# A gated mix of two spectral filters on one core: exchanging real and imaginary parts by DMA, gate rows from a constant column, gate sums over two engines

## The chip, the cores and the metric

The kernel runs on one core of one Trainium2 chip. The core has five engines that run their own instruction queues in order and meet at semaphores: PE (TensorE, matrix products from SBUF into PSUM), DVE (VectorE, elementwise work), ACT (ScalarE, functions and copies, here most copies out of PSUM), POOL (GpSimd, small elementwise work) and SP (SyncE, which here only issues DMAs). A DMA that an engine issues moves data on 16 shared DMA engines. PSUM has 8 banks of 512 fp32 columns, numbered 0 to 7.

The metric is the device time of one execution in microseconds (us), as the median of several runs. The profile is one further execution, recorded instruction by instruction; its span runs from the first instruction to the last.

## The reference

Two spectral filters are applied to the same input and mixed row by row with a gate:

```python
def _A_ref(x, w_r, w_i):          # _B_ref is the same
    X = rfft2(x.astype(float32), axes=(-2, -1))
    X = X * (w_r + 1j * w_i)
    return irfft2(X, s=(S, D), axes=(-2, -1)).astype(bfloat16)

x = A_x                                               # (1, 2048, 1024) bf16
g = sigmoid((x * gate_w).sum(-1, keepdims=True))      # one gate per row
return g * _A_ref(x, A_w_r, A_w_i) + (1 - g) * _B_ref(x, B_w_r, B_w_i)
```

The weights are 2048 x 513 each, real and imaginary, for A and B. Both filters share one forward transform, because their input is the same.

## The kernel before

The transform is written as matrix products with constant tables. The 2048 rows are split as 32 x 64: row 64 n1 + n2. SBUF holds 128 partitions with 16 rows of x each, so x arrives in 8 chunks of two rows per partition.

**Loads.** SP issues all large DMAs in one list (L264 to L291): table M, the chunks of x, the gate weights `gw` (one row of 1024 sent to all partitions, into RB), tables F2 and CK, and then the weights in 8 blocks W(0) to W(7) by `wblock`. Blocks 0 to 6 go to R_W, four DMAs each. Block 7 goes into R_M, over table M, in four pairs of DMAs (1539 and 513 columns); each of these lists all keys ("M", c) as written, so by the rule of `Prog.add` each waits for the one before it.

**Stage 1** (`stage1(c)`, c = 0 to 3, chunks 2c and 2c+1): transform over n1 and folding of columns. DVE copies reversed halves of x into RING (L314), PE runs 32 matmuls of 256 columns, and `evict1` (L340) takes four PSUM groups into R_F: three by ACT, the fourth, for step c-1, by DVE. A gate sum `zred(c)` (L305: x row times gate weights, summed into one column of ZS) stands on DVE in each step.

**Stages 2 and 4** are one loop over 16 slots i. `stage2(i)`: 8 matmuls of 512 columns (L378) give the spectrum along d; ACT evicts it as CS(i) into RING (L381; 3 buffers); POOL copies one column to STAR. `stage4(i)`: 8 matmuls (L399) finish the row transform twice, once with the constants in normal order (sw = 0) and once with real and imaginary columns swapped (sw = 1). ACT evicts both, X(0, i) and X(1, i), into RING (L402; 2 buffers each). Then DVE forms two products with the weights (L413), 2048 columns each: `product` for sw = 0 goes to R_A, where x has been, and for sw = 1 to R_W, over the weights of block j-1, with j = i // 2. Real and imaginary parts lie in partitions 2k and 2k+1. The program order on each engine is that of the calls: stage2(i+1), wsave on POOL for even i, stage4(i), and in iterations 0 to 5 two further `zred`.

**The gate.** `gate_diag(r)` (L355) lets POOL write the identity times column r of ZS, a 128 x 128 block of DZ; two per iteration for i below 8. `gate_rows` (called in iterations 10 and 11) multiplies them by a matrix of ones on PE (L362), which spreads each sum over all partitions, and ACT applies the sigmoid (L367) into DZ. After the loop DVE makes from it the masks GM in RING (L467).

**Stages 5 to 7.** Before stage 5, U5 replaces block 7 and F2 in R_M by a DMA; `star` and PST treat the single last column. Stage 5 (L526, 32 groups of 16 matmuls, PSUM slots of two banks used in turn, evicted by ACT and DVE alternately at L535) transforms back over the rows; it needs all products. `rbgen` (L480) makes, from U5 and GM, the right-hand sides of `stage6` (L558) in seven buffers `rbs`; `stage7` (L571) transforms back along d, DVE adds and subtracts the halves (L579), and SP stores 16 outputs.

Semaphores: `Prog.add` takes for each operation the keys it reads (r), rewrites (w: waits for all earlier readers and writers) and adds to (a: waits for earlier readers). Waits are inserted from these, and engines never reorder.

Of the kernel before, what the change touches and what calls it, by code (L numbers as in the profile page):

```python
# [205 lines left out]
def bass_gated_mix__spectral_gfnet__spectral_gfnet__prompt_kernel(nc, A_x, A_w_r, A_w_i, B_x, B_w_r, B_w_i, gate_w, out):  # L206
# [71 lines left out]
    def wblock(j):  # L278
        t, base = (R_W, 4112 * (j + 1)) if j < 7 else (R_M, 0)
        for f in range(2):  # L280
            for ri in range(2):
                w = wsrc[f, ri]
                d0 = base + 2052 * f
                if j < 7:
                    parts = [(d0, 2052, [[(29 - 4 * j) * 513, 2], [1, 1026]], 2 * j + 1)]
                else:
                    parts = [(d0, 1539, [[1, 1539]], 15), (d0 + 1539, 513, [[1, 513]], 0)]
                for do, n, dims, k in parts:
                    dma("sp", AP(t, ri * t.shape[1] + do, [[2 * t.shape[1], 64], [1, n]]),
                        AP(w.tensor, w.offset + k * 513, [[32 * 513, 64]] + dims),  # L290
                        w=[("M", c) for c in range(4)] + [("M-", c) for c in range(4)] if j == 7 else [], a=[("W", j)])  # L291
# [10 lines left out]


    def zred(r):
        P.add("dve", lambda e: e.tensor_tensor_reduce(  # L305
            out=sl(RB, 1024, [(1, 1024)]), in0=sl(R_A, XO + r * 1024, [(1, 1024)]), in1=sl(RB, GWo, [(1, 1024)]),
            scale=1.0, scalar=0.0, op0=ALU.mult, op1=ALU.add, accum_out=ZS[:, r:r + 1]),
            r=[("x", r // 2), "gw"], w=["zjunk"], a=[("z", r)])
# [45 lines left out]
    def gate_diag(r):  # L354
        P.add("pool", lambda e: e.tensor_scalar(out=sl(DZ, r * 128, [(1, 128)]), in0=sl(CK, IDo, [(1, 128)]),  # L355
                                                scalar1=ZS[:, r:r + 1], scalar2=None, op0=ALU.mult),
              r=[("z", r), "CK"], a=["DZ"])

    def gate_rows(h):
        b0 = 2 * h  # L360
        for q in range(2 * h, 2 * h + 2):
            P.add("pe", lambda e, q=q: e.matmul(ps((b0 + q % 2) * 512, [(1, 512)]), sl(CK, ONo, [(1, 128)]),  # L362
                                                sl(DZ, q * 512, [(1, 512)]), start=True, stop=True),
                  r=["DZ", "CK"], w=[bank(b0 + q % 2)])
# [21 lines left out]
    def stage4(i):  # L386
        t = order[i]
        kind = 0 if t else 1
        ro = CSO + (i % 3) * 1028
        for sw in range(2):  # L390
            b0 = 4 + 2 * sw
            for pm in range(2):
                for m in range(2):
# [5 lines left out]
                    P.add("pe", lambda e, o=o, lh=lh, rh=rh, m=m: e.matmul(o, lh, rh, start=(m == 0), stop=(m == 1)),  # L399
                          r=["CK", ("CS", i % 3)], w=[bank(b0 + pm)])  # L400
# [1 line left out]
            P.add("act", lambda e, xo=xo, b0=b0: e.activation(sl(RING, xo, [(1, 1024)]), ps(b0 * 512, [(1, 1024)]), ACT.Copy),  # L402
                  r=[bank(b0), bank(b0 + 1)], w=[("X", sw, i % 2)] + ALLX)
# [2 lines left out]
        for sw in range(2):
            xin = sl(RING, (XAO if sw == 0 else XSO) + (i % 2) * 1024, [(0, 2), (512, 2), (1, 512)])
            win = sl(wt, w0, [(2052, 2), (dpm, 2), (1, 512)])
            dst = sl(R_A if sw == 0 else R_W, 4 * i * RW, [(2 * RW, 2), (RW, 2), (1, 512)])
            free = [("x", c) for c in range(8)] if sw == 0 and i >= 8 else []  # L410
            if sw == 1 and j > 0:
                free = [("W", j - 1)]
            P.add("dve", lambda e, d=dst, a=xin, b=win: e.tensor_tensor(out=d, in0=a, in1=b, op=ALU.mult),  # L413
                  r=[("X", sw, i % 2), ("W", j)], a=[("prod", sw)] + free)
# [60 lines left out]

    def rbgen(r):
        t, so = rbs[r % 7]
        for cp in range(2):
            for ri in range(2):
# [3 lines left out]
                    in1=sl(RING, r * 256, [(64, 4), (32, 2), (1, 32)]), op=ALU.mult),  # L483
# [171 lines left out]
```

## Time and profile before

| | us |
|---|---|
| median of 3 runs | 180.57 |
| range of the runs | 179.12 to 180.71 |
| the profiled execution's own time | 180.38 |
| its span | 178.5 |

| engine | busy us | share of the span |
|---|---|---|
| PE, matmuls | 152.0 | 85% |
| DVE | 119.0 | 67% |
| ACT | 110.1 | 62% |
| POOL | 44.9 | 25% |

The profile names an instruction by its line in the kernel file (L378), its engine, and its tiles as output<-input. In a timeline a row reads: start, time from there to the end, engine, line, operation, tiles, count, and in brackets how long the engine had been idle and what ended that. In a table of groups, a row ends with total busy time, mean nanoseconds of one, and the idle time before. An instruction's duration is longer than the distance to the next where the two overlap. Time outside the span (180.38 less 178.5) belongs to the execution but to no instruction.

### The profile page before, as it was taken

How to read it: one execution, taken by the hardware profiler on the slowest of the kernel's cores; microseconds unless marked ns; L12 is line 12 of the kernel's file. 1: busy time of each engine (PE TensorE's matmuls, PEld its weight loads, DVE VectorE, ACT ScalarE, POOL GpSimd, SP SyncE). 2: the span in 40 equal slices, each digit the busy share in tenths (PEclk: the TensorE clock that was granted, in tenths of full speed). 3: DMA queues.
4: the chain of work that ended last, by engine and by line, in shares of the span. 5: the costliest groups of instructions: out<-in, count | busy, mean ns of one | idle time of the engine just before them, and what ended most of it. 6: DMA issues, size and time to landing. Idle time of an engine off the chain costs nothing. (4 is left out here: it accounts for less than half of the span.)

```text
span 178.5 us, 3235 instructions
## 1 busy us (share of the span) xinstructions
PE 152.0 (85%) x1295; PEld 99.0 (55%) x1308; DVE 119.0 (67%) x192; ACT 110.1 (62%) x121; POOL 44.9 (25%) x55
## 2 busy tenths in 40 slices
PE   0789969999997723999985799999978999999991
PEld 0568834444442201344434799999966666656640
DVE  0168722999999992055779277888852787765463
ACT  4359837888876660498992545476556665565550
POOL 0000005899999997001014000000000000000000
PEclk9999999999999996599997899999999999999999
DMA  5999999991221000000003900000051313322323
GB/s 161 300 417 431 400 383 387 389 379 39 59 56 51 15 0 0 0 4 2 0 0 62 385 26 4 0 4 0 4 174 64 118 62 120 118 87 93 118 112 124
DMA packets 9295, 22.97 MB, mean 129 GB/s; under 512 B 1216, under 2 KB 1600, under 8 KB 8896
## 3 DMA queue, kind: packets, MB, share of 16 engines
q1 hardware_dynamic: 9136, 22.76, 34.9%
q8 instruction: 10, 0.16, 0.4%
q14 instruction: 5, 0.04, 0.1%
q10 hardware_dynamic: 144, 0.00, 0.0%
HBM read 18.57 MB, written 4.19 MB: 127 GB/s over the span
## 5 line engine op out<-in xcount | busy, mean ns | idle before, releaser
L402 ACT ACTIVATE RING<-PS 128x1024 bf16<-128x1024 f32 x32 | 32.8, 1024 | 7.4 <-DVE R_A L413 3.8
L399 PE MATMUL PS<-RING,CK 128*128 128x512 bf16 (+1 forms) x123 | 31.2, 384 | 3.0 <-ACT RING L402 2.6
L526 PE MATMUL PS<-CK,R_A 128*128 128x128 bf16 x256 | 32.4, 228 | 1.2 <-DVE R_A L413 1.2
L526 PE MATMUL PS<-CK,R_W 128*128 128x128 bf16 x256 | 32.3, 228 | 0.9 <-DVE R_W L413 0.9
L378 PE MATMUL PS<-R_M,R_F 128*128 128x512 bf16 x127 | 31.6, 395 | 1.6 <-issue 1.6
L526 PEld LDWEIGHTS PS<-CK,R_A 128*128 128x128 bf16 x256 | 31.4, 145 | 1.3 <-DVE R_A L413 1.3
L526 PEld LDWEIGHTS PS<-CK,R_W 128*128 128x128 bf16 x256 | 31.4, 145 | 1.0 <-DVE R_W L413 1.0
L579 DVE TENSOR_TENSOR R_A<-R_A,PS 128x512 bf16<-128x512 f32 x32 | 20.6, 684 | 15.3 <-ACT R_A L575 10.0
L571 PE MATMUL PS<-R_A 128*128 128x512 bf16 x121 | 29.2, 379 | 0.9 <-DMA R_A<-c_DI 0.6
L413 DVE TENSOR_TENSOR R_A<-RING,R_W 128x2048 bf16<-128x2048 bf16 x14 | 17.2, 1231 | 18.6 <-ACT RING L402 18.6
L355 POOL TENSOR_SCALAR DZ<-CK,ZS 128x128 bf16<-128x128 bf16 x16 | 29.3, 1839 | 0.0
L562 ACT ACTIVATE R_A<-PS 128x1024 bf16<-128x1024 f32 x16 | 16.3, 1024 | 16.7 <-PE PS L558 16.7
L399 PEld LDWEIGHTS PS<-RING,CK 128*128 128x128 bf16 x128 | 12.1, 99 | 20.3 <-ACT RING L402 6.3
L378 PEld LDWEIGHTS PS<-R_M,R_F 128*128 128x128 bf16 x128 | 12.9, 101 | 17.8 <-issue 3.8
L332 PE MATMUL PS<-R_M,R_A 128*128 128x256 bf16 x64 | 16.3, 298 | 6.3 <-DVE RING L314 5.6
L305 DVE CUSTOM_DVE_ANT_0 RB<-R_A,RB 128x1024 bf16<-128x1024 bf16 x16 | 19.8, 1235 | 2.8 <-DMA RB<-in_gate_w_dram 2.6
L381 ACT ACTIVATE RING<-PS 128x1024 bf16<-128x1024 f32 x16 | 16.5, 1029 | 7.5 <-PE PS L378 6.6
L571 PEld LDWEIGHTS PS<-R_A 128*128 128x128 bf16 x128 | 11.9, 98 | 12.3 <-DMA R_A<-c_DI 0.5
L383 POOL COPY STAR<-RING 128x1 bf16<-128x1 bf16 x16 | 6.8, 426 | 46.9 <-ACT RING L381 46.9
L413 DVE TENSOR_TENSOR R_W<-RING,R_W 128x2048 bf16<-128x2048 bf16 x14 | 17.5, 1250 | 0.0
L332 PE MATMUL PS<-R_M,RING 128*128 128x256 bf16 x64 | 16.3, 298 | 0.0
L535 ACT ACTIVATE R_F<-PS 128x1024 bf16<-128x1024 f32 x8 | 8.2, 1024 | 10.4 <-PE PS L526 10.4
(55 smaller groups left out, 167.5 us busy)
## 6 DMA issues: line engine op xcount, KB each, us to landing
R_A<-in_A_x_dram SPq DMA_DIRECT2D x8, 512.0 KB, 8.8
out_dram<-R_A SPq DMA_DIRECT2D x16, 256.0 KB, 2.0
R_M<-c_U SPq DMA_DIRECT2D x1, 2048.0 KB, 7.6
R_W<-in_A_w_r_dram SPq DMA_DIRECT2D x7, 256.5 KB, 10.8
R_W<-in_A_w_i_dram SPq DMA_DIRECT2D x7, 256.5 KB, 10.4
R_W<-in_B_w_r_dram SPq DMA_DIRECT2D x7, 256.5 KB, 9.6
R_W<-in_B_w_i_dram SPq DMA_DIRECT2D x7, 256.5 KB, 9.7
R_M<-c_F SPq DMA_DIRECT2D x1, 1024.0 KB, 13.4
```

Of the source, the lines that this page charges most:

```text
L305: P.add("dve", lambda e: e.tensor_tensor_reduce(out=sl(RB, 1024, [(1, 1024)]), in0=sl(R_A, XO + r * 1024, [(1, 1024)]), in1=sl(RB, GWo, [( ...
L332: P.add("pe", lambda e, o=o, lh=lh, rh=rh, h=h: e.matmul(o, lh, rh, start=(h == 0), stop=(h == 1)), r=[("x", 2 * c + q // 2), ("M", c), (" ...
L355: P.add("pool", lambda e: e.tensor_scalar(out=sl(DZ, r * 128, [(1, 128)]), in0=sl(CK, IDo, [(1, 128)]), scalar1=ZS[:, r:r + 1], scalar2=No ...
L378: P.add("pe", lambda e, o=o, lh=lh, rh=rh, j=j: e.matmul(o, lh, rh, start=(j == 0), stop=(j == 3)), r=["F1", "F2"], w=[bank(b0 + cs)])
L381: P.add("act", lambda e: e.activation(sl(RING, ro, [(513, 2), (1, 512)]), ps(b0 * 512, [(512, 2), (1, 512)]), ACT.Copy), r=[bank(b0), bank ...
L399: P.add("pe", lambda e, o=o, lh=lh, rh=rh, m=m: e.matmul(o, lh, rh, start=(m == 0), stop=(m == 1)), r=["CK", ("CS", i % 3)], w=[bank(b0 + ...
L402: P.add("act", lambda e, xo=xo, b0=b0: e.activation(sl(RING, xo, [(1, 1024)]), ps(b0 * 512, [(1, 1024)]), ACT.Copy), r=[bank(b0), bank(b0 ...
L413: P.add("dve", lambda e, d=dst, a=xin, b=win: e.tensor_tensor(out=d, in0=a, in1=b, op=ALU.mult), r=[("X", sw, i % 2), ("W", j)], a=[("prod ...
L526: P.add("pe", lambda e, o=o, t=t, l0=l0, ab=ab: e.matmul(o, sl(t, l0, [(257, 128)]), sl(CK, KIAo if ab == 0 else KIBo, [(1, 128)]), start= ...
L562: P.add("act", lambda e, s=src, d=dst: e.activation(d, s, ACT.Copy), r=[bank(b0), bank(b0 + 1)], w=[("Y", r)], after=[last5])
L571: P.add("pe", lambda e, o=o, lh=lh, rh=rh, q=q: e.matmul(o, lh, rh, start=(q == 0), stop=(q == 3)), r=[("Y", r), "DI"], w=[bank(b0 + ri)])
L579: P.add("dve", lambda e, od=od, h=h: e.tensor_tensor(out=od, in0=es, in1=ps((b0 + 1) * 512, [(1, 512)]), op=ALU.add if h == 0 else ALU.sub ...
```

## The change

- **Exchange.** In iterations 0 to 14, stage 4 runs only sw = 0. The swapped copy is made by two DMAs on SP, SBUF to SBUF: odd partitions of XA(i) to even partitions of XS(i) and the reverse, 64 partitions of 1024 columns each. XA has 4 buffers in RING, XS has 3, in RB and DZ. Iteration 15 still computes both on PE. PSUM banks 4 to 7 alternate by iteration.
- **Order of the products.** `product(0, i)` stays in iteration i; `product(1, i-2)` follows it, two iterations after its exchange. The loop ends with (1,13), (0,15), (1,15), (1,14).
- **Weight loads.** `wloads` lists 32 loads (block, filter, part). The first 20 (blocks 0 to 4) are issued ahead of the loop; then two loads in each of iterations 0 to 5, behind the exchange of that iteration on SP.
- **Gate sums.** For rows 0 to 11, DVE multiplies x by the gate weights in place (`zpair`, two rows at a time, in stage 1's steps 1 to 3), and ACT sums each row with a Copy that has an accumulator output (`zsum`): three ahead of stage 2, nine inside the loop after the XA eviction of iterations 0, 1, 3, 4, 6, 7, 9, 10 and 12. Rows 12 to 15 keep the fused sum on DVE, now in place, after stage 1.
- **Gate rows.** The diagonals on POOL are gone. DVE copies ZS to ZB in bf16 after product(1,12); PE multiplies a column of ZB, read with step 0 as a 128 x 128 stationary operand, by the identity, 16 matmuls of 128 columns; the four sigmoids write into RING. All of it stands behind the loop, after XST.
- **Start.** A memset on DVE and ten matmuls of 512 columns on the zeros stand ahead of stage 1. The gate weights are loaded before chunk 1 of x, where they were loaded before chunk 2.
- **Buffers.** `rbs` uses other places, GM lies at column 2056 of RING, and stage 5 starts with PSUM slot 2 where it started with slot 1. Frees of x by the products go by the chunks they overlap.

```diff
-        if c == 2:
+        if c == 1:
             dma("sp", sl(RB, GWo, [(1, 1024)]), AP(gate_w.tensor, gate_w.offset, [[0, 128], [1, 1024]]), w=["gw"])
...
-    def wblock(j):
+    def wload(j, f, ri):
...
+            dma("sp", AP(t, ri * t.shape[1] + do, [[2 * t.shape[1], 64], [1, n]]),
+                AP(w.tensor, w.offset + k * 513, [[32 * 513, 64]] + dims),
+                w=[("M", c) for c in range(4)] + [("M-", c) for c in range(4)] if j == 7 else [], a=[("W", j)])
+
+    wloads = [(j, f, ri) for j in range(8) for f in range(2) for ri in range(2)]
...
+    P.add("dve", lambda e: e.memset(sl(R_F, 0, [(1, 512)]), 0.0), w=["F1"])
+    for n in range(10):
+        P.add("pe", lambda e: e.matmul(ps(3584, [(1, 512)]), sl(R_F, 0, [(1, 128)]), sl(R_F, 0, [(1, 512)]), start=True, stop=True),
+              r=["F1"], w=[bank(7)])
+
+    def zpair(k):
+        xs = sl(R_A, XO + k * 2048, [(1024, 2), (1, 1024)])
+        P.add("dve", lambda e: e.tensor_tensor(out=xs, in0=xs, in1=sl(RB, GWo, [(0, 2), (1, 1024)]), op=ALU.mult),
+              r=["gw"], w=[("x", k)])
+
+    def zsum(r):
+        xs = sl(R_A, XO + r * 1024, [(1, 1024)])
+        P.add("act", lambda e: e.activation(xs, xs, ACT.Copy, accum_out=ZS[:, r:r + 1]), r=[("x", r // 2)], a=["z"])
...
             evict1(c - 1, 3, "dve")
-        zred(c)
+            zpair(2 * c - 2)
+            zpair(2 * c - 1)
...
-    for j in range(8):
-        wblock(j)
+    for r in range(12, 16):
+        zred(r)
+    for n in range(20):
+        wload(*wloads[n])
...
+    def gate_rows():
+        for q in (1, 2, 3, 0):
+            for r in range(4 * q, 4 * q + 4):
+                P.add("pe", lambda e, r=r: e.matmul(ps(r * 128, [(1, 128)]), sl(ZB, r, [(0, 128)]), sl(CK, IDo, [(1, 128)]),
+                                                    start=True, stop=True), r=["ZB", "CK"], w=[bank(q)])
+            src = ps(q * 512, [(128, 4), (1, 4), (4, 32)])
+            P.add("act", lambda e, q=q, s=src: e.activation(sl(RING, q * 512, [(1, 512)]), s, ACT.Sigmoid, scale=SM[:, 0:1]),
+                  r=[bank(q), "SM"], a=["G"] + [("CS", i) for i in range(3)])
...
-        for sw in range(2):
-            b0 = 4 + 2 * sw
+        xo = XAO + (i % 4) * 1024
+        xt, xs = xsb[i % 3]
+        for sw in range(2 if i == 15 else 1):
+            b0 = 4 + 2 * ((i + sw) % 2)
...
+        if i < 15:
+            for ri in range(2):
+                src = AP(RING, (1 - ri) * RING.shape[1] + xo, [[2 * RING.shape[1], 64], [1, 1024]])
+                dst = AP(xt, ri * xt.shape[1] + xs, [[2 * xt.shape[1], 64], [1, 1024]])
+                dma("sp", dst, src, r=[("XA", i % 4)], w=[("XS", i % 3)] if ri == 0 else [], a=[("XS", i % 3)] if ri else [])
...
+    zat = {0: 3, 1: 4, 3: 5, 4: 6, 6: 7, 7: 8, 9: 9, 10: 10, 12: 11}
+    for r in range(3):
+        zsum(r)
     stage2(0)
     for i in range(16):
-        if i in (10, 11):
-            gate_rows(i - 10)
         if i + 1 < 16:
             stage2(i + 1)
         if i % 2 == 0:
             wsave(i // 2)
         stage4(i)
-        if i < 6:
-            zred(4 + 2 * i)
-            zred(5 + 2 * i)
-        if i < 8:
-            gate_diag(2 * i)
-            gate_diag(2 * i + 1)
+        if i in zat:
+            zsum(zat[i])
+        for n in range(20 + 2 * i, min(22 + 2 * i, 32)):
+            wload(*wloads[n])
+        if i == 15:
+            product(1, 13)
+        product(0, i)
+        if i >= 2:
+            product(1, i - 2 if i < 15 else 15)
+        if i == 14:
+            P.add("dve", lambda e: e.tensor_copy(ZB[:], ZS[:]), r=["z"], w=["ZB"])
+    product(1, 14)
...
-    slot = 1
+    slot = 2
```

More of the change, by code (lines that the diff above doesn't have):

```diff
@@ L275, in bass_gated_mix__spectral_gfnet__spectral_gfnet__prompt_kernel @@
               r=[("M", c)], w=[("M-", c)])
-    def wblock(j):
+    def wload(j, f, ri):
         t, base = (R_W, 4112 * (j + 1)) if j < 7 else (R_M, 0)
[L280 to L291, printed above, removed]
+        w = wsrc[f, ri]
+        d0 = base + 2052 * f
+        if j < 7:
+            parts = [(d0, 2052, [[(29 - 4 * j) * 513, 2], [1, 1026]], 2 * j + 1)]
+        else:
+            parts = [(d0, 1539, [[1, 1539]], 15), (d0 + 1539, 513, [[1, 513]], 0)]
+        for do, n, dims, k in parts:
+            dma("sp", AP(t, ri * t.shape[1] + do, [[2 * t.shape[1], 64], [1, n]]),
+                AP(w.tensor, w.offset + k * 513, [[32 * 513, 64]] + dims),
+                w=[("M", c) for c in range(4)] + [("M-", c) for c in range(4)] if j == 7 else [], a=[("W", j)])
+    wloads = [(j, f, ri) for j in range(8) for f in range(2) for ri in range(2)]
     def wrow(j, a):
@@ L400, in stage4 @@
                           r=["CK", ("CS", i % 3)], w=[bank(b0 + pm)])
-            xo = (XAO if sw == 0 else XSO) + (i % 2) * 1024
-            P.add("act", lambda e, xo=xo, b0=b0: e.activation(sl(RING, xo, [(1, 1024)]), ps(b0 * 512, [(1, 1024)]), ACT.Copy),
-                  r=[bank(b0), bank(b0 + 1)], w=[("X", sw, i % 2)] + ALLX)
+            dst, key = (sl(RING, xo, [(1, 1024)]), ("XA", i % 4)) if sw == 0 else (sl(xt, xs, [(1, 1024)]), ("XS", i % 3))
+            P.add("act", lambda e, d=dst, b0=b0: e.activation(d, ps(b0 * 512, [(1, 1024)]), ACT.Copy),
+                  r=[bank(b0), bank(b0 + 1)], w=[key] + ALLX)
@@ L404, in stage4, with product @@
+        if i < 15:
[3 more added lines that the diff above has]
+                dma("sp", dst, src, r=[("XA", i % 4)], w=[("XS", i % 3)] if ri == 0 else [], a=[("XS", i % 3)] if ri else [])
+    def product(sw, i):
         j = i // 2
         wt, w0, dpm = wrow(j, i % 2)
[L406 to L414, printed above, removed]
+        xt, xo = (RING, XAO + (i % 4) * 1024) if sw == 0 else xsb[i % 3]
+        xin = sl(xt, xo, [(0, 2), (512, 2), (1, 512)])
+        win = sl(wt, w0, [(2052, 2), (dpm, 2), (1, 512)])
+        dst = sl(R_A if sw == 0 else R_W, 4 * i * RW, [(2 * RW, 2), (RW, 2), (1, 512)])
+        free = []
+        if sw == 0 and i >= 8:
+            k0, k1 = (max(0, 4 * i * RW - XO) // 2048, ((4 * i + 4) * RW - 1 - XO) // 2048)
+            free = [("x", k) for k in range(k0, k1 + 1)]
+        if sw == 1 and j > 0:
+            free = [("W", j - 1)]
+        P.add("dve", lambda e: e.tensor_tensor(out=dst, in0=xin, in1=win, op=ALU.mult),
+              r=[("XA", i % 4) if sw == 0 else ("XS", i % 3), ("W", j)], a=[("prod", sw)] + free)
@@ L482, in rbgen @@
                     in0=sl(R_M, r * 512 + cp * 64 + ri * 32, [(128, 4), (0, 2), (1, 32)]),
[L483 removed]
+                    in1=sl(RING, GMo + r * 256, [(64, 4), (32, 2), (1, 32)]), op=ALU.mult),
                     r=["U5", "GM"], w=[("RB", r % 7, cp, ri)], a=rbk[r] if r < 7 else [])
```

32 lines of the change are left out of this document (11 added, 21 removed).

## The prediction, made before the changed kernel was run

> **What bounds the kernel now.** I read first the table by stretches, because the mean over the span (PE 85% busy) hides a stage in which the engine at the limit changes. Columns: stretch, its length, busy time of PE, PEld, DVE, ACT and POOL, granted clock, DMA share, GB/s.
>
> ```profile
> span 178.5 us, 3235 instructions
> 31.00:48.40 17.40, 17.29 (x80) 7.87 (x81) 17.26 (x23) 15.46 (x16) 16.70 (x12) 1.00 0.62 224
> 48.40:63.00 14.60, 12.50 (x56) 4.89 (x55) 14.53 (x18) 9.75 (x11) 14.60 (x12) 1.00 0.15 42
> 63.00:70.00 7.00, 0.56 (x3) 0.07 (x1) 5.28 (x5) 2.66 (x3) 7.00 (x7) 0.89 0.00 0
> 70.00:77.00 7.00, 6.99 (x21) 2.69 (x22) 0.12 (x1) 3.36 (x5) 0.95 (x7) 0.62 0.00 0
> 77.00:93.50 16.50, 15.70 (x71) 6.80 (x72) 11.36 (x10) 15.14 (x16) 1.40 (x8) 1.00 0.01 1
> ```
>
> The loop of stages 2 and 4 runs from 24 to 96 us. PE, DVE and POOL are all nearly full up to 48, then DVE and POOL are; from 63 to 70 PE stands still, and from 70 to 77 it works at a granted clock of 0.62; after that PE and ACT are full together. The timeline, engine by engine, says why:
>
> ```profile
> 63.66 5.01 POOL L355 TENSOR_SCALAR DZ<-CK,ZS 128x128 bf16<-128x128 bf16 x2
> 70.01 1.04 PE L362 MATMUL PS<-DZ,CK 128*128 128x512 bf16 x2 [6.45 <-POOL DZ L355]
> 70.84 3.62 PE L378 MATMUL PS<-R_M,R_F 128*128 128x512 bf16 x8
> 80.38 1.89 PE L378 MATMUL PS<-R_M,R_F 128*128 128x512 bf16 x8
> 83.83 1.89 PE L378 MATMUL PS<-R_M,R_F 128*128 128x512 bf16 x8
> 88.07 1.23 DVE L413 TENSOR_TENSOR R_A<-RING,R_W 128x2048 bf16<-128x2048 bf16 x1 [1.05 <-ACT RING L402]
> 89.21 1.22 DVE L413 TENSOR_TENSOR R_W<-RING,R_W 128x2048 bf16<-128x2048 bf16 x1
> 90.43 4.44 ACT L402 ACTIVATE RING<-PS 128x1024 bf16<-128x1024 f32 x4
> 94.91 1.22 DVE L413 TENSOR_TENSOR R_W<-RING,R_M 128x2048 bf16<-128x2048 bf16 x1
> 96.18 0.32 PE L526 MATMUL PS<-CK,R_W 128*128 128x128 bf16 x1 [0.87 <-DVE R_W L413]
> ```
>
> PE waits 6.45 us for POOL's diagonals, then runs its next eight matmuls in 3.62 us where eight take 1.89. Undisturbed, an iteration of 16 matmuls is 83.83 − 80.38 = 3.45 us, so one 512-column matmul is 0.216. A product is 89.21 − 88.07 = 1.14 apart, an ACT eviction (4.44 − 1.02)/3 = 1.14. Stage 5 starts when the last product ends (96.13); from 96.18 to the end of the span, 82.3 us, PE bounds and the change touches only a buffer and a bank number.
>
> **The change part by part.**
>
> *Removed.* Half of stage 4 in 15 of 16 iterations: 60 matmuls (13 us of PE), 15 evictions (17 us of ACT). The 16 diagonals on POOL with the wait above. PE needs 12 × 0.216 = 2.6 us an iteration, DVE two products, 2.3, ACT two evictions plus, in 9 iterations, a gate sum. So ACT becomes the busiest engine of the loop, until something waits.
>
> *Start of the loop.* DVE now does two 2048-wide gate products (zpair) in each of stage 1's steps 1 to 3, where it did one gate sum.
>
> ```profile
> 11.99 0.43 DVE L314 COPY RING<-R_A 128x1024 bf16<-128x1024 bf16 x1 [0.85 <-DMA R_A<-in_A_x_dram]
> 12.34 1.22 DVE L340 CAST R_F<-PS 128x1024 bf16<-128x1024 f32 x1
> 13.47 1.21 DVE L305 CUSTOM_DVE_ANT_0 RB<-R_A,RB 128x1024 bf16<-128x1024 bf16 x1
> 14.61 0.76 DVE L314 COPY RING<-R_A 128x1024 bf16<-128x1024 bf16 x2
> 22.95 1.22 DVE L340 CAST R_F<-PS 128x1024 bf16<-128x1024 f32 x1 [1.13 <-PE PS L332]
> 24.49 3.40 PE L378 MATMUL PS<-R_M,R_F 128*128 128x512 bf16 x15 [1.58 <-issue]
> 20.33 2.85 ACT L340 ACTIVATE R_F<-PS 128x1024 bf16<-128x1024 f32 x3 [0.64 <-PE PS L332]
> ```
>
> No row shows zpair; the product of the same size and kind gives 1.15. From the fourth chunk of x (its copy starts at 11.99, on a DMA) DVE has no gap any more: 12.35, then twice (eviction 1.14 + zpair 2.3 + copies 0.78), then 1.14 + 2.3, then the last eviction 1.22: 25.4 instead of 24.17. PE starts stage 2 at 25.7, ACT is free of stage 1 at 24.3 instead of 23.2. The four gate sums left to DVE then run to 30.4 and are hidden, since no product can start before 31.6.
>
> The ten warm-up matmuls and the memset cost and gain nothing: step 1 waits for the chunk at 11.99 however fast step 0 was. Moving the gate-weight load forward delays x's second chunk by about 2 us at most, hidden by the same wait (exposed, 2 us).
>
> *Gate sums on ACT.* No row shows an ACT sum. Bounds from rows:
>
> ```profile
> L274 ACT ACTIVATE R_M<-R_M 128x512 bf16<-128x512 bf16 x4 | 2.3, 622 | 4.1 <-DMA R_M<-c_M 4.1
> L263 ACT ACTIVATE JNK<-JNK 128x1 f32<-128x1 f32 x1 | 0.2, 202 | 0.0
> L402 ACT ACTIVATE RING<-PS 128x1024 bf16<-128x1024 f32 x32 | 32.8, 1024 | 7.4 <-DVE R_A L413 3.8 <-DVE R_W L413 0.4 <-PE PS L399 0.3
> L305 DVE CUSTOM_DVE_ANT_0 RB<-R_A,RB 128x1024 bf16<-128x1024 bf16 x16 | 19.8, 1235 | 2.8 <-DMA RB<-in_gate_w_dram 2.6
> ```
>
> 1024 columns take 1.02; a separate read of the accumulator would be a [128x1] instruction of up to 0.20, partly overlapped. Low end 1.0, high end 1.4, taken 1.2. In the Trainium skill, ScalarE: Activation LUTs, the rules for kernel authors say that multiplications and additions belong on VectorE rather than ScalarE, and the section on what a table load costs prices an ACTIVATE at 186 ns + 0.833 ns per column. As an estimate from that page an ACT sum is 1.04 us without the accumulator, and the sum below would come 1 us lower. The rule speaks against this edit, and the rows agree with it: a sum was 1.24 on DVE and is now 0.57 + 1.2 over both.
>
> An XA eviction waits for two DMAs more than before. 1.14 is the low end, taken 1.25, high end 1.36, since these evictions with several waits already stand 1.14 apart where stage 1's three in 2.85 stand 0.92 apart.
>
> ACT: three sums from 24.3 to 27.9, CS0 and CS1 to 30.3, XA0 to 31.6 (after PE's first two stage 2 and stage 4); then up to XA4's end 3 sums, 4 CS and 4 XA, 3.6 + 4.6 + 5.0 = 13.2: XA4 is ready at 44.7.
>
> *Exchange and weight loads share SP's queue.* This decides the result. An exchange waits on SP for its XA, and behind it stand the loads of weight blocks 5 to 7. Block 7 goes into R_M in eight parts, each of which rewrites the same keys and so waits for the one before to land. SP's timeline and the DMA table (KB, us to landing):
>
> ```profile
> 33.23 9.78 SPq L257 DMA_DIRECT2D R_M<-in_A_w_r_dram  x2
> 44.63 3.05 SPq L257 DMA_DIRECT2D R_M<-in_A_w_i_dram  x2
> 49.30 3.15 SPq L257 DMA_DIRECT2D R_M<-in_B_w_r_dram  x2
> 54.15 3.13 SPq L257 DMA_DIRECT2D R_M<-in_B_w_i_dram  x2
> R_M<-in_A_w_i_dram SPq DMA_DIRECT2D x1, 192.4 KB, 2.6
> R_M<-in_A_w_i_dram SPq DMA_DIRECT2D x1, 64.1 KB, 2.1
> R_W<-in_A_w_r_dram SPq DMA_DIRECT2D x7, 256.5 KB, 10.8
> out_dram<-R_A SPq DMA_DIRECT2D x16, 256.0 KB, 2.0
> ```
>
> Today each pair of parts costs 49.30 − 44.63 = 4.7 us, and nothing waits behind them. In the changed order they stand after exchanges 4 and 5. Exchange 4 is issued at 44.7 (two issues, 1.0), the first part at 45.7; seven landings later (4 × 2.6 + 3 × 2.1 = 16.7, and 0.4 for the exchange ahead in the queue) the eighth is issued at 62.8, with exchange 5 slipped in at 53.7. Exchange 6, whose XA was ready at 50.7, is issued only at 63.3. An exchange half is 128 KB: between 2.0 and 2.6 to landing, taken 2.4, plus 0.5 for the second issue: it lands at 66.2. Blocks 5 and 6 are loaded long before use.
>
> Who waits: DVE at product(1,6), with product(0,9) and all later ones behind it; ACT at XA10, which overwrites what exchange 6 reads; PE through full banks. Behind 66.2 DVE has 17 products, (1,6), then (0,9) to (0,15) and (1,7) to (1,15). At 1.15 they take 19.6, plus 0.4 of waits for the last XA: the last product, (1,14), ends at **86.2**. ACT's own chain from XA10 on, 6 XA, 4 CS, 2 sums and XS15, is 15.6, to 81.8, and fits beside this; so does PE's.
>
> *Tail.* PE finishes stage 4 at about 80.5, before XS15's eviction; the gate rows' 16 small matmuls follow when the copy ZB is done (81.7), the four sigmoids (0.69 each) end before 85.5 on ACT; stage 5's groups behind them on PE would wait for the products anyway, as would GM on DVE. If that cover is gone they cost 2.5. PE again stands about 2.7 us before stage 5, as now:
>
> ```profile
> 93.50:96.20 2.70, 0.64 (x11) 0.41 (x9) 2.70 (x5) 1.36 (x3) 0.00 (x0) 0.92 0.00 0
> 97.00:99.00 2.00, 2.00 (x22) 2.00 (x20) 0.90 (x2) 0.97 (x1) 1.23 (x2) 0.50 0.95 221
> ```
>
> so stage 5 begins at half clock, already contained in the 82.3.
>
> **Sum.** 86.2 + 82.3 = 168.5 us of span. The profiled execution of 178.5 took 180.38, 1.9 around the span and 0.2 below the median of 180.57: **170.4**. The loop gives 96.1 − 86.2 = 9.9.
>
> **The rivals.**
> *A, the block-7 queue does not bite* and ACT bounds to the end. From XA0 at 31.6: 9 sums, 14 CS and XA1 to XA14 are 10.8 + 16.0 + 17.5, to 75.9; then six products, (0,14), (1,12), (1,13), (0,15), (1,15), (1,14), 6.9: 82.8, so 167.0; with ACT's low ends (12 × 0.2 + 15 × 0.11 less) 163.0. It needs exchange 6 down by XA10's natural turn near 60.4, 5.8 us sooner, that is 0.8 us off each of the seven landings. Against it: the rows of the parts keep their pace on a queue that holds nothing else.
> *B, ACT is dearer*: sums 1.4 and XA 1.36 move XA4 and all behind it by 6 × 0.2 + 5 × 0.11 = 1.8: 172.2. Exchanges at 5 us to landing instead of 2.4 would move exchange 6 by 2.6: 173.0; both together 174.8.
> *C, slower than before: exchanges land as late as weight loads do.* With three XS buffers, exchange i+3 cannot start before product(1,i), and product(1,i) not before exchange i lands. From 31.6, five rounds (exchanges 0, 3, 6, 9, 12) of landing + 0.5 + two products, then five more products (5.8): with 10.8 us to landing 31.6 + 5 × 13.6 + 5.8 = 105.4, a time of 189.6. It decides from a landing of about 9 us. The weight rows have that, under a full queue; but the queue has run empty once the first part of block 7 has landed (the row of 9.78 us ends with the second part's issue, at 43.0), and parts then land in 2.1 to 2.6. The Trainium skill, DMA: Bandwidth & Descriptors, on queues, rings and completion order, says that each engine consumes a queue's descriptors in ring order. By that rule exchange 0, issued behind twenty weight loads, is late too, and later ones are not; the 10.8 us row agrees.
>
> **How the numbers follow.** Forecast 0.60 (168 to 173), A 0.20 (163 to 167.5), B 0.15 (172 to 176), C 0.04, no visible change 0.01. The range 164.5 to 175.5 leaves out half of A's low end, B's high end and C. All but C and the last are faster by over 1%, which is about what a measurement of this kernel tells from no change: faster 0.95, same 0.02, slower 0.03.
>
> **What would show it.** Right: SP's R_M loads from about 46 to 65 in pairs of 4.7 us with exchange 6 behind them; DVE idle for some 7 us before product(1,6), then full for 20; ACT idle before XA10; stage 5 starting at 86. Stage 2 starting at 24.5 rather than 25.7 refutes the stage 1 step; ACT sums outside 1.0 to 1.4 the ACT step. Exchanges landing in over 5 us, or no DVE gap after 55, would make the forecast wrong.

## The result, and the profile after

| | before | after |
|---|---|---|
| median, us | 179.84 (178.24 to 180.71, 4 runs) | 170.62 (170.13 to 172.16, 4 runs) |
| ratio | | 0.951, 95% interval 0.941 to 0.961 |
| profiled execution, us | 180.38 | 170.13 |
| its span, us | 178.5 | 168.2 |

The changed kernel is faster by 9.2 us. The forecast was 170.4. The table by stretches of the changed kernel, read first again (stretch, length, busy time of PE, PEld, DVE, ACT, POOL, granted clock, DMA share, GB/s):

```profile
24.20:46.00 21.80, 20.06 (x94) 9.04 (x95) 15.74 (x18) 20.41 (x28) 3.91 (x13) 1.00 0.96 336
46.00:58.50 12.50, 12.11 (x55) 5.20 (x55) 7.90 (x7) 11.47 (x16) 4.33 (x8) 1.00 0.32 96
58.50:66.00 7.50, 3.41 (x15) 1.19 (x13) 0.34 (x1) 1.01 (x2) 0.48 (x3) 0.94 0.27 88
66.00:85.60 19.60, 11.63 (x62) 5.12 (x62) 19.58 (x20) 15.57 (x20) 6.75 (x8) 0.76 0.28 105
83.00:85.60 2.60, 0.34 (x2) 0.16 (x2) 2.60 (x5) 1.43 (x3) 0.00 (x0) 0.50 0.00 0
85.60:89.00 3.40, 3.40 (x32) 3.40 (x33) 1.68 (x4) 1.03 (x1) 1.81 (x2) 0.50 0.75 207
```

The last two rows, which overlap the one above them, come in with the clock below. Until 58.5 ACT is the full engine (20.41 of 21.80, 11.47 of 12.50). From 58.5 to 66.0 DVE and ACT stand (PE too, from 62.3 on), and from 66.0 to 85.6 DVE has no gap at all: 19.58 of 19.60. The old hole from 63 to 70, when PE waited for POOL's diagonals, is gone; in nearly the same place there is a new one of 7.5 us. The timeline of SP in the changed kernel shows its cause. SP issues block 7 of the weights (R_M) and the exchanges (DZ or RB<-RING) in one order:

```profile
43.92 1.16 SPq L259 DMA_DIRECT2D DZ<-RING  x2
45.20 3.56 SPq L259 DMA_DIRECT2D R_M<-in_A_w_r_dram  x2
50.44 3.14 SPq L259 DMA_DIRECT2D R_M<-in_A_w_i_dram  x2
53.75 1.13 SPq L259 DMA_DIRECT2D DZ<-RING  x2
55.22 3.10 SPq L259 DMA_DIRECT2D R_M<-in_B_w_r_dram  x2
59.98 3.23 SPq L259 DMA_DIRECT2D R_M<-in_B_w_i_dram  x2
63.37 1.13 SPq L259 DMA_DIRECT2D RB<-RING  x2
```

Rows 1, 4 and 7 are exchanges 4, 5 and 6. Between them stand the eight parts of block 7, each waiting for the one before to land, the eighth issued at 62.7 (near the end of the row that starts at 59.98). Exchange 6 has to wait behind it until 63.37. Who waits for exchange 6 is in the timeline of DVE in the changed kernel (the bracket gives the idle time and what ended it):

```profile
57.62 1.22 DVE L439 TENSOR_TENSOR R_A<-RING,R_W 128x2048 bf16<-128x2048 bf16 x1
66.02 1.23 DVE L439 TENSOR_TENSOR R_W<-RB,R_W 128x2048 bf16<-128x2048 bf16 x1 [7.18 <-DMA RB<-RING]
67.17 1.22 DVE L439 TENSOR_TENSOR R_A<-RING,R_W 128x2048 bf16<-128x2048 bf16 x1
...
84.31 1.22 DVE L439 TENSOR_TENSOR R_W<-DZ,R_M 128x2048 bf16<-128x2048 bf16 x1
```

and in the timeline of ACT:

```profile
58.49 1.02 ACT L394 ACTIVATE RING<-PS 128x1024 bf16<-128x1024 f32 x1
66.09 1.02 ACT L417 ACTIVATE RING<-PS 128x1024 bf16<-128x1024 f32 x1 [6.58 <-DMA RB<-RING]
```

DVE stands 7.18 us at product(1,6), ACT 6.58 us at XA10, both until the exchange lands. (For exchange 5, which stands between the parts too, DVE had waited 3.39 us, up to 56.47.) Then 17 products follow one another in 19.5 us, to 85.53, and stage 5 takes 82.6 us from there to the end of the span.

### The profile page after: what moved, and what is told of

It reads as the page before. It is cut to its first block, busy times and chain, and to the rows that moved or that the text cites. A ratio compares the mean times of both kernels' runs of the same rounds, so it can differ in the third digit from the quotient of the medians.

```text
span 168.2 us, 3201 instructions
## 1 busy us (share of the span) xinstructions
PE 141.6 (84%) x1259; PEld 93.9 (56%) x1270; DVE 110.9 (66%) x176; ACT 106.0 (63%) x130; POOL 17.6 (10%) x39
## 5 line engine op out<-in xcount | busy, mean ns | idle before, releaser
L561 PE MATMUL PS<-CK,R_W 128*128 128x128 bf16 x256 | 32.5, 229 | 2.0 <-DVE R_W L439 2.0
L561 PE MATMUL PS<-CK,R_A 128*128 128x128 bf16 x256 | 32.7, 229 | 0.5 <-DVE R_A L439 0.5
L561 PEld LDWEIGHTS PS<-CK,R_W 128*128 128x128 bf16 x256 | 31.5, 145 | 2.1 <-DVE R_W L439 2.1
L561 PEld LDWEIGHTS PS<-CK,R_A 128*128 128x128 bf16 x256 | 31.5, 145 | 0.8 <-DVE R_A L439 0.8
L391 PE MATMUL PS<-R_M,R_F 128*128 128x512 bf16 x126 | 30.3, 384 | 1.6 <-DVE R_F L358 1.5
L597 ACT ACTIVATE R_A<-PS 128x1024 bf16<-128x1024 f32 x16 | 16.3, 1024 | 16.8 <-PE PS L593 16.8
L414 PE MATMUL PS<-RING,CK 128*128 128x512 bf16 (+1 forms) x66 | 18.1, 395 | 8.1 <-ACT RING L394 7.8
L439 DVE TENSOR_TENSOR R_A<-RING,R_W 128x2048 bf16<-128x2048 bf16 x14 | 17.1, 1223 | 7.2 <-ACT RING L417 7.2
L417 ACT ACTIVATE RING<-PS 128x1024 bf16<-128x1024 f32 x16 | 16.4, 1025 | 8.6 <-DMA RB<-RING 6.6
L350 PE MATMUL PS<-R_M,R_A 128*128 128x256 bf16 x64 | 14.7, 278 | 3.8 <-DVE RING L331 2.5
L394 ACT ACTIVATE RING<-PS 128x1024 bf16<-128x1024 f32 x16 | 16.4, 1023 | 1.4 <-PE PS L391 1.0
L414 PEld LDWEIGHTS PS<-RING,CK 128*128 128x128 bf16 x68 | 6.2, 99 | 18.2 <-ACT RING L394 10.9
L350 PE MATMUL PS<-R_M,RING 128*128 128x256 bf16 x64 | 14.7, 277 | 0.0
L570 DVE CAST R_F<-PS 128x1024 bf16<-128x1024 f32 x8 | 9.8, 1224 | 6.6 <-PE PS L561 6.6
L396 POOL COPY STAR<-RING 128x1 bf16<-128x1 bf16 x16 | 7.3, 455 | 63.5 <-ACT RING L394 63.5
L570 ACT ACTIVATE R_W<-PS 128x1024 bf16<-128x1024 f32 x8 | 10.0, 1245 | 5.7 <-PE PS L561 5.7
L439 DVE TENSOR_TENSOR R_W<-DZ,R_W 128x2048 bf16<-128x2048 bf16 x9 | 11.0, 1221 | 3.4 <-DMA DZ<-RING 3.4
```

Of the source, the lines that this page charges most:

```text
L350: P.add("pe", lambda e, o=o, lh=lh, rh=rh, h=h: e.matmul(o, lh, rh, start=(h == 0), stop=(h == 1)), r=[("x", 2 * c + q // 2), ("M", c), (" ...
L391: P.add("pe", lambda e, o=o, lh=lh, rh=rh, j=j: e.matmul(o, lh, rh, start=(j == 0), stop=(j == 3)), r=["F1", "F2"], w=[bank(b0 + cs)])
L394: P.add("act", lambda e: e.activation(sl(RING, ro, [(513, 2), (1, 512)]), ps(b0 * 512, [(512, 2), (1, 512)]), ACT.Copy), r=[bank(b0), bank ...
L417: P.add("act", lambda e, d=dst, b0=b0: e.activation(d, ps(b0 * 512, [(1, 1024)]), ACT.Copy), r=[bank(b0), bank(b0 + 1)], w=[key] + ALLX)
L439: P.add("dve", lambda e: e.tensor_tensor(out=dst, in0=xin, in1=win, op=ALU.mult), r=[("XA", i % 4) if sw == 0 else ("XS", i % 3), ("W", j) ...
L561: P.add("pe", lambda e, o=o, t=t, l0=l0, ab=ab: e.matmul(o, sl(t, l0, [(257, 128)]), sl(CK, KIAo if ab == 0 else KIBo, [(1, 128)]), start= ...
```

## The experiments

All times in the table are medians; each ratio is against the kernel before, run on the same chip beside that kernel, with its 95% interval.

| run | what it is | us | kernel before beside it | ratio |
|---|---|---|---|---|
| w7_unchained | after, block 7's parts not chained | 163.21 | 179.28 | 0.907 (0.900 to 0.914) |
| w7_spread | after, one chained part per iteration 4 to 11 | 163.13 | 179.28 | 0.906 (0.899 to 0.913) |
| no_exchange | after, swapped copy on PE again | 177.98 | 179.28 | 0.988 (0.981 to 0.996) |
| before_zb_rows | before, with the new gate rows only | 169.41 | 179.28 | 0.941 (0.933 to 0.949) |
| no_warmup_gw_back | after, without the edits at the start | 171.20 | 180.50 | 0.951 (0.943 to 0.958) |
| spread_zpair_later | w7_spread, fewer zpair in stage 1 | 162.04 | 180.50 | 0.899 (0.891 to 0.907) |
| sums_all_dve | w7_spread, all gate sums fused on DVE | 165.94 | 180.50 | 0.921 (0.913 to 0.929) |
| shift_sums_lag1 | w7_spread, two sums to DVE, products one iteration earlier | 160.00 | 180.50 | 0.888 (0.882 to 0.895) |
| best_keep_clock | shift_sums_lag1, PE kept busy ahead of stage 5 | 158.18 | 179.16 | 0.881 (0.875 to 0.886) |
| after_keep_clock | after, PE kept busy ahead of stage 5 | 169.33 | 179.16 | 0.941 (0.937 to 0.946) |

### Is it block 7's chain on SP? (w7_unchained, w7_spread)

The theory is that of the prediction: exchange 6 is late because SP's queue is held by the chained parts. The rival is that DVE or ACT would need the time in any case. Two different edits take the hold away: one leaves out the keys that chain the parts, the other keeps the chain but puts one part behind each exchange.

```diff
# w7_unchained: only the first of the eight parts lists the M keys
-                w=[...] if j == 7 else [], a=[("W", j)])
+                w=[...] if (j, f, ri, k) == (7, 0, 0, 15) else [], a=[("W", j)])
# w7_spread
-        for n in range(20 + 2 * i, min(22 + 2 * i, 32)):
+        for n in range(20 + 2 * i, min(22 + 2 * i, 28)):
             wload(*wloads[n])
+        if 4 <= i < 12:
+            wload(*wloads[28 + (i - 4) // 2], only=(i - 4) % 2)
```

> The changed kernel, but only the first of block 7's eight parts waits for table M's readers; the other seven are issued without waiting for one another. Queue theory (the parts' waits on SP hold exchange 6 back by about 12 us, and from its landing 17 products on DVE set the end): exchange 6 is issued right after its XA, near 50, DVE has no gap over 2 us, ACT runs on at 2.8 us an iteration (the changed kernel's profile: 8.46 us for three iterations from 40.2 to 48.6), XA14 ends near 71, six products later, near 78, the loop ends: about 163 us (162 to 165). Rival, ACT's own chain bounds the loop and covers the delay: within 1 us of the changed kernel, about 170.6.

> The changed kernel with the same eight chained parts of block 7, but one part behind the exchange of each of the iterations 4 to 11, so that each part's predecessor has landed by the time it comes up on SP. Queue theory: the waits cost nothing when nothing is due behind them, so the same as with the parts unchained, about 163 us (162 to 165), with block 7 complete near 70, before product(0,14). Rival, the parts cost by their number or by the traffic they make beside the exchanges: within 1 us of the changed kernel, about 170.6.

Both take 163 us, 7.5 us less than the changed kernel. SP's timeline in w7_unchained:

```profile
45.50 1.16 SPq L259 DMA_DIRECT2D R_M<-in_A_w_r_dram  x2
46.71 1.34 SPq L259 DMA_DIRECT2D R_M<-in_A_w_i_dram  x2
48.21 1.13 SPq L259 DMA_DIRECT2D DZ<-RING  x2
49.38 1.23 SPq L259 DMA_DIRECT2D R_M<-in_B_w_r_dram  x2
50.66 1.24 SPq L259 DMA_DIRECT2D R_M<-in_B_w_i_dram  x2
52.06 1.13 SPq L259 DMA_DIRECT2D RB<-RING  x2
```

A pair of parts now costs 1.2 to 1.3 us of SP and no wait; exchange 6 goes out at 52.06 instead of 63.37. In w7_spread it goes out at 49.38. What DVE waits for then is in the groups by line of w7_spread (count, busy us, mean ns, idle time before and what ended it):

```profile
L439 DVE TENSOR_TENSOR R_A<-RING,R_W 128x2048 bf16<-128x2048 bf16 x14 | 17.2, 1226 | 10.1 <-ACT RING L417 10.1
L439 DVE TENSOR_TENSOR R_W<-DZ,R_W 128x2048 bf16<-128x2048 bf16 x9 | 11.0, 1220 | 0.0
```

The products that read an exchanged copy (second row) never wait any more; those that read XA wait for ACT, 10.1 us in ten waits. So with the queue free ACT bounds the loop, as rival A had it. The chain of eight landings is shown as the cause of the hole, and 7.5 us as its price.

### Which part of the change brings the gain? (before_zb_rows, no_exchange)

One kernel has the new gate rows alone, on the kernel before; the other has everything but the exchange.

```diff
# before_zb_rows: before, without gate_diag
+        if i == 5:
+            P.add("dve", lambda e: e.tensor_copy(ZB[:], ZS[:]), ...)
...
+    gate_rows()          # the new ones, behind XST; slot = 2
# no_exchange: after; the second line is the condition of the two exchange DMAs
-        for sw in range(2 if i == 15 else 1):
+        for sw in range(2):
...
-        if i < 15:
+        if i < 0:
```

> The kernel before with one part of the change alone: no diagonals on POOL, gate sums copied to ZB in bf16 after the last of them, gate rows by ZB columns against the identity behind the loop. If PE's wait for POOL and the slow clock after it are what this part removes: stage 4 of iteration 10 ends near 67 where it ended near 76, DVE catches up in the meantime, about 9 us less: 171 us (169 to 174). Rival, DVE's sums in iterations 0 to 5 bound the loop and the wait only hid that: 176 to 180 us.

> The changed kernel without the exchange: stage 4 computes the swapped copy on PE in every iteration and ACT evicts it into the same XS buffers; gate sums, weight loads and order of products stay as changed. If ACT is what the exchange relieves: 49 evictions at 1.12 us and 9 sums at 1.04 us from 28 on end near 92, the last products near 95: about 179 us (176 to 182). Rival, PE's 3.45 us an iteration bounds (ACT's sums fit beside it): the loop ends near 26 + 55 + 5 = 86, about 170.

The gate rows alone give 9.9 us, as much as the whole change. In the profiled executions the last product ends 9.8 us earlier than in the kernel before (86.3 and 96.1), and stage 5, which starts at full clock here, takes 81.0 us instead of 82.3. So a part of the gain lies in stage 5; in the changed kernel stage 5 gains nothing (82.6). The table by stretches of before_zb_rows, over the old hole and behind it:

```profile
63.00:70.00 7.00, 7.00 (x34) 3.16 (x33) 6.99 (x7) 6.32 (x7) 3.56 (x4) 1.00 0.00 0
70.00:77.00 7.00, 6.95 (x33) 3.13 (x33) 4.91 (x5) 6.32 (x7) 0.67 (x4) 1.00 0.01 2
```

PE is busy 7.00 of 7.00 us where it was busy 0.56, and the granted clock stays at 1.00 where it was 0.62. The same two stretches of no_exchange:

```profile
63.00:70.00 7.00, 6.42 (x31) 2.71 (x30) 4.73 (x4) 6.48 (x9) 0.27 (x2) 1.00 0.00 1
70.00:77.00 7.00, 5.85 (x26) 2.36 (x26) 4.15 (x4) 6.57 (x8) 0.59 (x4) 1.00 0.01 2
```

Here ACT is the fullest engine and DVE has room: with three evictions an iteration and the moved sums ACT is late, and in the whole execution the products that read XA wait 25.3 us for it, where in before_zb_rows they wait 10.1. In medians, the step from before_zb_rows to no_exchange (sums to ACT, order of the products, weight loads and the start) costs 8.6 us; these parts were not taken one by one. The exchange gives back 14.8 where the chain is spread (to 163.13), and 7.4 where it is not (to the changed kernel's 170.62, measured in a session of its own). So the exchange is worth much, but as built all of it pays for that step and for the wait on SP's queue: the changed kernel is no faster than before_zb_rows. What the new gate rows are worth inside the changed kernel stays open, since no run puts the diagonals back there.

### The edits at the start (no_warmup_gw_back, spread_zpair_later)

The first kernel has no memset and no ten matmuls, and loads the gate weights ahead of chunk 2 again. The second is w7_spread with one zpair in each stage 1 step instead of two; the rest follows behind stage 1.

```diff
# spread_zpair_later
-            zpair(2 * c - 2)
-            zpair(2 * c - 1)
+            zpair(c - 1)
...
-    for r in range(12, 16):
+    for k in range(3, 6):
+        zpair(k)
+    for r in range(12, 14):
         zred(r)
...
+        if i < 2:
+            zred(14 + i)
```

> The changed kernel without the ten matmuls on zeros and their memset, and with the gate weights loaded again before chunk 2 of x. If these two edits are hidden behind x's fourth chunk, as the sum has it: stage 2 starts within 0.4 us of 13.6 us after the copy of that chunk, and the time is that of the changed kernel within 1 us, about 170.6. Rival, the warmed clock shortens stage 1: stage 2 starts some 2 us later against that copy, 172.5.

> The kernel with block 7's parts spread, and DVE's gate products in stage 1 cut from two to one per step; the other three, and two of the four fused sums, stand behind stage 1, the last two sums in iterations 0 and 1. If the two products per step are what delays stage 2: it starts 12.5 us after the copy of x's fourth chunk, as in the kernel before, where the changed kernel has 13.6, and the time falls by the same 1.1 us, to 162.0 (161.3 to 162.7). Rival, DVE, pushed full behind stage 1, starts its products later and gives it back: 163.1.

Without the edits at the start the time is the same within the intervals. The fourth chunk's copy on DVE then stands at 12.05, and PE starts stage 2 at 25.67, 13.6 us behind it, as with them (12.70 and 26.29). With three zpair in stage 1 instead of six the distance is 12.4 (12.40 to 24.85): the second zpair of each step delays stage 2 by some 1.1 us. The time of spread_zpair_later is 1.1 lower than that of w7_spread, but the intervals of the two ratios overlap, so that alone shows no gain.

### Where the gate sums belong (sums_all_dve, shift_sums_lag1)

```diff
# sums_all_dve: no zpair, no zsum; four zred behind stage 1, and
+        if i < 6:
+            zred(2 * i)
+            zred(2 * i + 1)
# shift_sums_lag1: one zpair a step; rows 10 and 11 on DVE; product(1, i - 1) from i = 9
-    zat = {0: 3, 1: 4, 3: 5, 4: 6, 6: 7, 7: 8, 9: 9, 10: 10, 12: 11}
+    zat = {0: 3, 1: 4, 3: 5, 4: 6, 6: 7, 7: 8, 9: 9}
...
+        if i in (0, 4, 7):
+            zred({0: 15, 4: 10, 7: 11}[i])
```

> The kernel with block 7's parts spread, and all 16 gate sums fused on DVE again (four behind stage 1, two in each of iterations 0 to 5), none on ACT and no gate products in stage 1. If the split over DVE and ACT is worth its price once the exchange has relieved PE and ACT: stage 2 starts 1.1 us sooner, but DVE then has 32 products at 1.14 and 12 sums at 1.23 from about 30.7, to near 82: 166.6 us (165 to 168). Rival, the waits DVE has for ACT (10 us in the spread kernel) take the sums in: 162.

> The kernel with block 7's parts spread, one gate product per step in stage 1, the sums of rows 10 and 11 moved from ACT to DVE (in iterations 4 and 7), and from iteration 9 on the swapped product one iteration behind its exchange in place of two. If ACT bounds the loop and DVE the tail: 1.1 us less from the start, 2 x 1.04 from ACT, one product, 1.1, from the tail: 163.1 - 4.3 = 158.8 us (158 to 160.5). Rival, PE's 2.6 us an iteration or the exchange's landing takes over: 161 to 162.

With all sums on DVE the loop is bound by DVE. The stretches of sums_all_dve:

```profile
48.00:63.00 15.00, 13.97 (x65) 6.05 (x65) 15.00 (x18) 9.79 (x11) 9.12 (x10) 1.00 0.28 95
63.00:70.00 7.00, 5.78 (x32) 2.38 (x32) 7.00 (x7) 5.12 (x5) 4.58 (x5) 1.00 0.51 177
```

DVE is busy all the time, ACT for two thirds of it; in w7_spread ACT is the full one (14.32 of the same 15.00, DVE 12.43). Between the two lies a better split: shift_sums_lag1, with ten sums on ACT and six on DVE, takes 160.0, though its products (1, i) come an iteration earlier too, and the two edits were not parted. That is 1.2 us more than its sum of 158.8: the last product ends 3.2 us earlier than in w7_spread (74.8 and 78.0), where the sum has 4.3. Which term fell short was not tried; from 48 to 63 PE, DVE and ACT are nearly full together (14.60, 14.47 and 13.98 us of 15.00). By the rules for kernel authors in the Trainium skill, ScalarE: Activation LUTs, additions and multiplications go to VectorE. Here that did not hold for all sixteen sums: with all of them on VectorE it is the full engine, and the time is 165.9 us, where it is 163.1 with twelve of them on ACT (the intervals of the two ratios just meet).

### The clock ahead of stage 5 (best_keep_clock, after_keep_clock)

Stage 5 took 82.6 us in the changed kernel and 83.4 in shift_sums_lag1, but 81.0 in before_zb_rows (from its first matmul on the last product to the end of the span). PE's timeline in the changed kernel, ahead of stage 5 (L377 are the gate rows, L561 stage 5):

```profile
78.99 0.34 PE L482 MATMUL PS<-STAR,CK 128*128 128x15 bf16 x8
81.04 0.84 PE L377 MATMUL PS<-CK,ZB 128*128 128x128 bf16 x12 [1.71 <-DVE ZB L474]
82.17 0.61 PE L377 MATMUL PS<-CK,ZB 128*128 128x128 bf16 x4 [0.29 <-ACT XST L489]
83.31 0.32 PE L561 MATMUL PS<-CK,R_A 128*128 128x128 bf16 x1 [0.53 <-DVE R_A L439]
85.58 0.32 PE L561 MATMUL PS<-CK,R_W 128*128 128x128 bf16 x1 [1.95 <-DVE R_W L439]
```

PE stands 1.71 us, works a little, and stands 1.95 us. The granted clock falls at about 82.2, between the two (rows in the last section), and is 0.50 from 83 to 89 (the last two rows of the first table), so stage 5 begins at half speed. Two kernels fill this time with matmuls whose result nothing reads, in one with an earlier copy ZB.

```diff
+    def keep(n):
+        for _ in range(n):
+            P.add("pe", lambda e: e.matmul(ps(3584, [(1, 512)]), sl(CK, 0, [(1, 128)]), sl(CK, 0, [(1, 512)]), ...), r=["CK"], w=[bank(7)])
# after_keep_clock: keep(8) ahead of gate_rows(), keep(12) behind it
# best_keep_clock: keep(18) behind gate_rows(), and
-        if i == 14:
+        if i == 11:
             P.add("dve", lambda e: e.tensor_copy(ZB[:], ZS[:]), ...)
```

> shift_sums_lag1 with the copy of the weights ZB at i = 11 instead of 14 and 18 more matmuls of 512 columns behind the gate rows, into a bank of PSUM that nothing reads, so that PE stays busy until stage 5. Theory: stage 5 took 83.4 us in shift_sums_lag1 because the granted clock was 0.50 from its start to 80 us after PE's idle ahead of it; with PE busy the clock stays at 1.00 and stage 5 takes 81.2 to 81.5 us as in before_zb_rows, so 160.0 - 2.0 = 158.0 us (157.3 to 158.8). Rival: the clock there does not hang on PE's idle, or the added matmuls hold stage 5 up by as much as they save: 160 us or more, with 0.50 still shown behind the gate rows.

> The changed kernel with 8 more matmuls of 512 columns between the last star product's matmuls and the gate rows and 12 behind the gate rows, into a bank of PSUM that nothing reads. Theory: the granted clock of 0.50 from 83 to 89 us comes from PE's idle before stage 5; with it filled stage 5 takes 81.2 us instead of 82.6 and the time is about 169.2 us (168.8 to 169.6). Rival: PE's idle does not set it: 170.6 us, with the row of 0.50 still there.

The stretches around the start of stage 5 (74.8 in both), in shift_sums_lag1:

```profile
70.00:74.80 4.80, 1.34 (x17) 1.03 (x17) 4.80 (x8) 2.82 (x6) 0.19 (x1) 0.83 0.04 15
74.80:80.00 5.20, 5.18 (x49) 5.18 (x50) 2.95 (x5) 1.02 (x1) 1.82 (x2) 0.50 0.80 274
```

and in best_keep_clock:

```profile
70.00:74.80 4.80, 4.32 (x26) 2.04 (x23) 4.80 (x5) 2.85 (x6) 0.41 (x1) 1.00 0.08 26
74.80:80.00 5.20, 4.08 (x68) 3.86 (x67) 3.11 (x6) 2.38 (x3) 1.85 (x2) 1.00 0.77 255
```

With PE kept busy the clock stays at 1.00, and PE does more in 4.08 busy us than it did in 5.18. The last product ends at the same time (74.8 and 74.9), and the span is 2.1 us shorter (156.1 and 158.2). In after_keep_clock stage 5 takes 81.1 us instead of 82.6; its last product ends 0.6 later than that of the changed kernel (exchange 6 already went out 0.6 later, at 64.01, long before the added matmuls), so the span is shorter by 0.9 only. The intervals of its ratio and of the changed kernel's overlap, so that small gain rests on the clock in the trace. best_keep_clock is the fastest of all kernels here, 158.18 us.

## Why the prediction was right, step by step

- **PE's wait for POOL and the half clock behind it go.** Right, and more than that: before_zb_rows shows that this one part carries a gain as large as that of the whole change. The prediction's sum could not show it, because it added up the new chain to its end and did not price the parts alone.
- **Stage 1.** Forecast +1.25 us, measured +1.1: stage 2 starts 13.6 us behind the fourth chunk's copy (26.29 and 12.70 in the rows below) where it stood 12.5 behind it. That it starts 0.6 later than forecast is due to the chunk, which came at 12.70 instead of 11.99, and that is in part the new order of the loads: the copy stands at 12.25 to 12.71 in the nine traces with the gate weights ahead of chunk 1, and at 11.99 to 12.35 in the three with them ahead of chunk 2. The timeline of DVE in the changed kernel:

```profile
12.70 0.43 DVE L331 COPY RING<-R_A 128x1024 bf16<-128x1024 bf16 x1 [0.85 <-DMA R_A<-in_A_x_dram]
...
14.18 2.35 DVE L313 TENSOR_TENSOR R_A<-R_A,RB 128x2048 bf16<-128x2048 bf16 x2
```

The second row is a pair of zpair, 2.3 us as priced. And the timeline of PE, with the start of stage 2:

```profile
26.29 3.40 PE L391 MATMUL PS<-R_M,R_F 128*128 128x512 bf16 x15 [1.55 <-DVE R_F L358]
```

- **Gate sums on ACT.** Forecast 1.2 us each between the ends 1.0 and 1.4; measured 1.04. XA evictions were put at 1.25; measured 0.92 where a sum follows and 1.14 where an eviction does (42.34 to 43.26 and 45.43 to 46.57 below). The timeline of ACT in the changed kernel:

```profile
24.89 1.07 ACT L318 ACTIVATE R_A<-R_A 128x1024 bf16<-128x1024 bf16 x1
25.83 0.21 ACT L318 ACTIVATION_READ_ACCUMULATOR R_A<-R_A 128x1 f32 x1
25.92 1.07 ACT L318 ACTIVATE R_A<-R_A 128x1024 bf16<-128x1024 bf16 x1
...
42.34 1.02 ACT L417 ACTIVATE RING<-PS 128x1024 bf16<-128x1024 f32 x1
43.26 1.05 ACT L318 ACTIVATE R_A<-R_A 128x1024 bf16<-128x1024 bf16 x1
44.21 0.19 ACT L318 ACTIVATION_READ_ACCUMULATOR R_A<-R_A 128x1 f32 x1
44.30 1.02 ACT L394 ACTIVATE RING<-PS 128x1024 bf16<-128x1024 f32 x1
45.43 1.02 ACT L417 ACTIVATE RING<-PS 128x1024 bf16<-128x1024 f32 x1
46.57 1.03 ACT L394 ACTIVATE RING<-PS 128x1024 bf16<-128x1024 f32 x1
```

The accumulator is read by an instruction of its own, 0.2 us, of which overlap leaves 0.09. The Trainium skill's estimate of 1.04 for a sum (ScalarE: Activation LUTs, on what a table load costs) agrees with the ACTIVATE of 1.05. That the distance to the next instruction is 1.04 too is chance: overlap takes 0.10 off, and the read of the accumulator puts 0.09 back. Two terms mis-sized, both too dear, brought exchange 4 out earlier than forecast (43.92 against 44.7) although stage 2 had started later. The next item shows where on SP the 0.8 us were lost again.
- **Exchange 4, block 7, exchange 6.** Forecast: first part at 45.7, eighth at 62.8, exchange 6 at 63.3. Measured: 45.20, 62.7, 63.37. From exchange 4 to the first part it took 0.3 us longer than forecast (1.3 against 1.0), and from the first part to the eighth 0.4 (17.5 against 17.1), so that of the 0.8 us by which exchange 4 was early 0.1 was left at the eighth part.
- **Landing of an exchange.** Forecast 2.4 us a half, measured 2.1 (the DMA table's median for DZ<-RING and RB<-RING, 128 KB each). Product(1,6) starts at 66.02 against 66.2. Rival C needed 9 us to be slower than the kernel before (by its own sum it would have set the end from 7 us on). The prediction had exchange 0 land late, behind the twenty weight loads; the slowest half into DZ, which holds exchanges 1 and 2 among others, took 4.8, and DVE waited for none before exchange 5.
- **The 17 products and the tail.** Forecast 19.6 + 0.4 to 86.2; measured 19.5 without a wait, to 85.53. Stage 5 was forecast at 82.3 and took 82.6: the half clock was there, as in the kernel before, but lasted 3.4 us into stage 5 (to 89.0) instead of 2.9 (to 99.1). PE stood longer ahead of it than the 2.7 us forecast: 1.71 + 0.29 + 0.53 + 1.95 = 4.5.
- **Warm-up matmuls and the gate weights' place.** Forecast nothing; no_warmup_gw_back shows nothing in the time within its interval. That the fourth chunk comes some 0.4 us later with the new order was not in the sum.
- **Rival A.** It did not come, but w7_unchained and w7_spread are that rival built: 163.1. Its working value of 167.0 was wrong because it rested on the two dear terms of ACT. Its low end of 163.0 was right in the time, but by two errors that cancel: the last product ended at 78.0 instead of 78.8, and stage 5 took 83.3 instead of 82.3, with the half clock lasting some 5 us into it (w7_spread).

The path was right; that the time agreed to 0.2 us is luck. Errors of up to 0.8 us in the chain's terms had both signs, the span came out 0.3 us shorter than forecast, and the median lies 0.5 above the profiled execution to which the sum was carried. What stays open: in no_warmup_gw_back exchange 4 went out 1.1 us earlier than in the changed kernel, but its two issues took 2.65 us where they took 1.16, so that block 7 began no earlier (45.59, and 45.20). The DMA engines had a share of 0.96 from 40.0 to 42.8 there and 0.82 in the changed kernel; whether that made the issues longer was not tried.

## What to carry to other kernels

When transfers on which an engine waits share a queue with transfers that wait for each other, work out the time at which each is issued, one by one: here eight landings in a row cost 7.5 us, and either leaving out the chain or putting one part behind each exchange brought it back. Take each part of a bundle alone before crediting the bundle: the gate rows alone brought what the whole change did, while the exchange only paid for the wait on SP's queue and for the edits that came with it, the sums moved to ACT among them. Give the work to the engine that is less full in that stage, and look at the granted clock at the start of a long stage that PE bounds; cheap matmuls in a short idle time ahead of it were worth 2 us.
